# Fourier mixing followed by a leaky-ReLU layer: the head reordered, VectorE's order fixed, and the first d=128 row spread by TensorE

## The chip, the cores and the metric

The kernel runs on one core of one Trainium2 chip. A core has a matrix engine (TensorE, in the profile PE, with its weight loads as PEld), a vector engine (VectorE, DVE), an activation engine (ScalarE, ACT), GpSimd (POOL) and a queue engine (SyncE, SP) that here only issues DMAs. SBUF is the on-chip memory of 128 partitions; PSUM holds the sums that TensorE writes, and only VectorE and ScalarE empty it here. The engines run side by side, each in the order in which its instructions stand, and meet at semaphores. The metric is the device time of one execution in microseconds.

## What is computed

A batch of 8 sequences of 3008 rows and 256 features goes through a two-dimensional Fourier transform of which the real part is kept, and then through two matrices with a leaky ReLU between them:

```python
X = np.fft.fft(x, axis=1)          # along the 3008 rows of each of 8 sequences
X = np.fft.fft(X, axis=2)          # along the 256 features
x = X.real.reshape(24064, 256)
h = x @ w_in                       # 256 x 2048
g = np.maximum(0.01 * h, h)
out = g @ w_out                    # 2048 x 256
```

x is float32. The two weight matrices arrive as float64, which no engine here computes with: the kernel reads each number as two 32-bit words and puts a float32 together from them.

## The kernel before

The rows are transformed by matmuls with cosine and sine tables, after the symmetries of the transform have been used to shorten them: rows that mirror each other are added, columns d and 256-d are added (cosine part) and subtracted (sine part), and the two halves of the sequence are added for even frequencies and subtracted for odd ones. That is the fold of x. Column 128, which has no mirror, is kept apart for all 8 sequences as nyx and transformed once per parity; its row is then needed on all 128 partitions. The feature transform is not done at all on x: it is folded into w_in (up_ps = feature table times w_in), so that wf takes its place, and wn is the row of wf that belongs to column 128.

A unit is one sequence and one parity, odd first; a unit has three chunks of about 251 frequency pairs. F = 2048 hidden features are 16 blocks of 128. For each chunk and each pair of hidden blocks there is an up step (four matmuls, four VectorE operations, one leaky ReLU) and a down step. The first two chunks use plain down steps of eight matmuls with w_out alone; all later chunks use seven products with sums of w_out blocks (wt), made on GpSimd.

```python
B, S, D, F = 8, 3008, 256, 2048
P = 128
PARITIES = (1, 0)
UW = [753, 752]      # frequencies of a unit, by parity
CW = 251             # of a chunk
NF = F // P          # 16 hidden blocks
NH = NF // 2
WN = 512             # columns of one piece of w_in
WB = WN // D         # hidden blocks of one piece of w_out: 2
```

The fold of x:

```python
    def fold_rows(t, h):

        a, z = t[:, h, 0], t[:, h, 1]
        nc.vector.tensor_tensor(a, a, z, op=ALU.add)
        lo, hi = a[:, :, 1:P], a[:, :, P + 1 : D]
        nc.vector.tensor_tensor(z[:, :, P + 1 : D], lo, hi, op=ALU.subtract)
        nc.vector.tensor_tensor(z[:, :, 1:P], lo, hi, op=ALU.add)
        nc.scalar.copy(z[:, :, 0:1], a[:, :, 0:1])
        nc.gpsimd.memset(z[:, :, P : P + 1], 0.0)

    def fold_halves(b, t):

        a, z = t[:, :, 0], t[:, :, 1]
        nc.vector.tensor_tensor(a[:, 0], z[:, 0], z[:, 1], op=ALU.add)
        nc.vector.tensor_tensor(a[:, 1], z[:, 0], z[:, 1], op=ALU.subtract)
        zs[b] = t
```

The weights. raw is a buffer for the float64 words; begin takes mantissa and exponent apart, with ScalarE scaling the exponent, and end puts the float32 together (the constructor, which issues the load, and the branch for float32 weights are left out):

```python
    # ... class Weights
        def begin(self):
            hi = self.word(I32, 1)
            self.power = work.tile([P, WN], F32, tag="power", bufs=2, name="power")
            man, power = self.dst, self.power
            man_i, power_i = man.bitcast(I32), power.bitcast(I32)
            v = nc.vector
            v.tensor_scalar(man_i, in0=hi, scalar1=0xFFFFF, scalar2=0x100000, op0=ALU.bitwise_and, op1=ALU.bitwise_or)
            v.tensor_scalar(power_i, in0=hi, scalar1=20, scalar2=0x7FF, op0=ALU.logical_shift_right, op1=ALU.bitwise_and)
            nc.scalar.activation(power, power_i, ACT.Relu, scale=-1.0, bias=inf[:, 0:1])
            nc.scalar.activation(power_i, power, ACT.Relu, scale=-(2.0**23), bias=inf[:, 1:2])

        def end(self):
            hi, lo = self.word(I32, 1), self.word(U32, 0)
            man, power = self.dst, self.power
            man_i, power_i = man.bitcast(I32), power.bitcast(I32)
            v = nc.vector
            v.scalar_tensor_tensor(man, in0=lo, scalar=2.0**-32, in1=man_i, op0=ALU.mult, op1=ALU.add)
            v.scalar_tensor_tensor(power_i, in0=hi, scalar=-(2**31), in1=power_i, op0=ALU.bitwise_and, op1=ALU.bitwise_or)
            v.scalar_tensor_tensor(man, in0=man, scalar=2.0**-20, in1=power, op0=ALU.mult, op1=ALU.mult)

    def convert(made):
        for w in made:
            w.begin()
        for w in made:
            w.end()
```

The products of the feature table with w_in, the path of wn through DRAM, and the loads of w_out:

```python
    def load_w_in(f0):
        n, made = w_in.shape[1] // F, []
        for a in range(2):
            # ... src: 128 rows of w_in, columns f0 to f0 + WN
            made.append(Weights(src, w))
        return made

    def fold_w_in(f0, made):

        for w in range(2):
            pt = up_ps()
            for a in range(2):
                nc.tensor.matmul(pt, lhsT=feat_sb[:, a, w * P : (w + 1) * P], rhs=made[a].dst, start=(a == 0), stop=(a == 1))
            nc.scalar.copy(wf[:, w, f0 : f0 + WN], pt)

    def spread_wn(f0):

        row = wn_dram[:, f0 : f0 + WN]
        nc.scalar.dma_start(row.rearrange("(o h) n -> o h n", o=1), wf[0:1, 1].rearrange("o (h n) -> o h n", h=2)[:, :, f0 : f0 + WN])
        at = f0 // P

        def rest():
            for h in range(2):
                nc.scalar.dma_start(wn[:, h * NH + at : h * NH + at + WN // P], row[h].rearrange("(q p) -> p q", p=P))
        return rest

    def load_w_out(f):
        made = []
        for h in range(2):
            at = (h * NH + f) * P
            src = w_out[at : at + WB * P, :].rearrange("(c p) d -> p c d", p=P)
            made.append(Weights(src, wo[:, h, f : f + WB, :].rearrange("p c d -> p (c d)")))
        return made
```

Column 128: its transform is written to DRAM and read back as a row on all partitions.

```python
    def nyquist(c):
        # ... rows of column 128 by parity
        sums = sequence(rows, B, 0, c)

        def rest():
            t = work.tile([P, UW[0]], F32, tag="mix0", bufs=2, name="nyq")
            butterfly(t, sums, B, 0, c)
            nc.sync.dma_start(nyq_dram[:, c, 0 : UW[c]], t[0:B, 0 : UW[c]])
        return rest

    def spread(u):

        b, c = u
        t = work.tile([P, UW[0]], F32, tag="nb", bufs=2, name="nb")
        nc.sync.dma_start(t[:, 0 : UW[c]], nyq_dram[b, c, 0 : UW[c]].partition_broadcast(P))
        spreads[u] = t
```

The up step, and the order of steps. The down step of a step follows three steps later in the text of the program (lag = 3); a scheduler then orders each engine's instructions.

```python
    # ...
    plain = 2
    steps = [(j, f) for f in range(NH) for j in range(plain)]
    steps += [(j, f) for j in range(plain, len(blocks)) for f in range(NH)]

    def up(j, f):
        b, c, at, n, _ = blocks[j]
        pt = [up_ps("cos_ps"), up_ps("sin_ps")]
        for blk in range(2):
            for h in range(2):
                fs = slice((h * NH + f) * P, (h * NH + f + 1) * P)
                nc.tensor.matmul(pt[blk][:, h * n : (h + 1) * n], lhsT=wf[:, blk, fs],
                                 rhs=mixed[b, c][blk][:, at : at + n], start=True, stop=True)
        cos = work.tile([P, 2 * CW], F32, tag="cos", bufs=3, name="cos")
        for h in range(2):
            hs = slice(h * n, (h + 1) * n)
            nc.vector.scalar_tensor_tensor(cos[:, hs], in0=spreads[b, c][:, at : at + n],
                                           scalar=wn[:, h * NH + f : h * NH + f + 1],
                                           in1=pt[0][:, hs], op0=ALU.mult, op1=ALU.add)
        g = work.tile([P, 2 * WN], F32, tag="g", bufs=5, name="g")[:, 0 : 4 * n].rearrange("p (r k) -> p r k", r=2)
        nc.vector.tensor_tensor(g[:, 0], cos[:, 0 : 2 * n], pt[1][:, 0 : 2 * n], op=ALU.add)
        nc.vector.tensor_tensor(g[:, 1], cos[:, 0 : 2 * n], pt[1][:, 0 : 2 * n], op=ALU.subtract)
        nc.scalar.activation(g, g, ACT.Lrelu)
        a = [[g[:, r, h * n : (h + 1) * n] for h in range(2)] for r in range(2)]
        if j < plain:
            hidden[j, f] = a
            return
        # ... (sums on GpSimd for the later chunks)
```

The head, up to the point from which everything repeats:

```python
    # ...
    w0 = load_w_in(0)
    nc.sync.dma_start(feat_sb, feat_tab.rearrange("(a p) n -> p a n", p=P))
    w2 = load_w_in(2 * WN)
    nc.sync.dma_start(nyx, x_nyq)
    t0 = load_x(0)
    for n in range(4):
        load_tab(nc.sync, n, 1)
    convert(w0)
    fold_w_in(0, w0)
    convert(w2)
    fold_w_in(2 * WN, w2)
    spread_wn(0)()
    fold_nyquist()
    fold_rows(t0, 0)
    fold_rows(t0, 1)
    fold_halves(0, t0)
    nyquist(1)()
    dft(units[0], 0)()
    spread(units[0])
    dft(units[0], 1)()
    at = 0

    def some_steps(n):
        nonlocal at
        for _ in range(n):
            step(at)
            at += 1

    o = load_w_out(0)
    convert(o)
    some_steps(plain)
    w = load_w_in(WN)
    convert(w)
    fold_w_in(WN, w)
    some_steps(plain)
    w = load_w_in(3 * WN)
    convert(w)
    fold_w_in(3 * WN, w)
    spread_wn(WN)()
    some_steps(plain)
    o = load_w_out(WB)
    for n in range(4):
        load_tab(nc.sync, n, 0)
    convert(o)
    for blk in range(2):
        fold_x_quarters(0, blk)
    some_steps(plain)
    nyquist(0)()
    spread(units[1])
    for f in range(2 * WB, NH, WB):
        o = load_w_out(f)
        convert(o)
        some_steps(plain)
        dft(units[1], f // WB - 2)()
    for f in range(0, NH, WB):
        combine_w_out(f)
    some_steps(len(steps) + lag - at)
```

## Time and profile before

| what | value |
|---|---|
| time, median of 3 | 1936.75 us (1935.41 to 1936.89) |
| span of the profiled execution | 1935.4 us |
| TensorE busy | 1909.9 us, 99% |
| VectorE busy | 1149.3 us, 59% |
| GpSimd busy | 1055.4 us, 55% |
| ScalarE busy | 468.6 us, 24% |
| DMA moved | 73.68 MB, mean 38 GB/s |

A line of the profile names an engine, a line of the kernel (L491), the tile that is written and those that are read, and a shape: 128x251 is 128 partitions by 251 elements. A float32 matmul appears as two records, so a group of eight matmuls counts 16. The chain is the work that ended last, followed backwards: what each piece of it waited for. "issue" in it is time in which the profile shows nothing that the engine waited for. A matmul's end in the profile is a model; the distance from one start to the next is the surer measure.

### The profile page before, as it was taken

Reading aid. Unit: us, or ns where it says so; the run is one execution under the profiler, and the core shown is the slowest. Engines: PE = TensorE matmul, PEld = TensorE weight load, DVE = VectorE, ACT = ScalarE, POOL = GpSimd, SP = SyncE. Lnnn points to the kernel's source line nnn. Section 1 sums busy time; section 2 is a strip of 40 time slices with the busy share of each in tenths; the row PEclk is TensorE's granted clock in tenths of the full one; section 3 lists DMA queues with packets and bytes.
Section 4 is the critical chain, followed back from the end, with each engine's and each line's share of the span. In section 5 each row is a group of like instructions: output and inputs, shape, how many; then the busy total and the mean of one; then the engine's idle time right before and its main releaser. Section 6 shows DMA issues by size and latency. Waiting matters only on the chain.

```text
span 1935.4 us, 24654 instructions
## 1 busy us (share of the span) xinstructions
PE 1909.9 (99%) x8988; PEld 1687.9 (87%) x8988; DVE 1149.3 (59%) x2245; ACT 468.6 (24%) x560; POOL 1055.4 (55%) x1508
## 2 busy tenths in 40 slices
PE   5999999999999999999999999999999999999999
PEld 3888888888888888888888888888888888888888
DVE  7975555585455845567555775457645585545554
ACT  3522222222222222222222222222222222222221
POOL 0115555575555755557555665557655575555554
PEclk8999999999999999999999999999999999999999
DMA  7220000020001100020000200002000020000000
GB/s 276 63 87 30 11 20 11 22 95 11 19 22 68 39 12 30 12 88 19 22 19 11 95 20 14 19 11 96 22 11 19 11 106 11 18 13 22 11 11 22
DMA packets 25600, 73.68 MB, mean 38 GB/s; under 512 B 4596, under 2 KB 17524, under 8 KB 23432
## 3 DMA queue, kind: packets, MB, share of 16 engines
q1 hardware_dynamic: 23360, 72.09, 10.1%
q8 instruction: 72, 1.18, 0.2%
q14 instruction: 48, 0.39, 0.1%
q10 hardware_dynamic: 2120, 0.02, 0.1%
HBM read 47.38 MB, written 24.71 MB: 37 GB/s over the span
## 4 chain that ended last, share of the span: by engine, by line
PE 98%; DMA 1%; DVE 0%; issue 0%; ACT 0%; SPq 0%; ACTq 0%; DVEq 0%
PE sum_ps L554 56%; PE cos_ps L491 17%; PE sin_ps L491 17%; PE sum_ps L534 3%; PE dft_ps L412 3%; PE dft_ps L402 2%; PE up_ps L357 1%; DMA raw<-in_w_in_dram 0%; DMA wn_dram<-wf 0%; DVE power L333 0%; DVE e L565 0%; DVE cos L496 0%; ACT g L502 0%; ACTq L369 0%; SPq L305 0%
## 5 line engine op out<-in xcount | busy, mean ns | idle before, releaser
L496 DVE SCALAR_TENSOR_TENSOR cos<-nb,wn,cos_ps 128x251 f32<-128x251 f32 (+1 forms) x768 | 330.6, 472 | 682.6 <-PE cos_ps L491 682.3
L502 ACT ACTIVATE g<-g 128x1004 f32<-128x1004 f32 (+1 forms) x384 | 399.2, 1039 | 1154.4 <-DVE g L501 1102.6
L509 POOL TENSOR_TENSOR s<-g 128x251 f32<-128x251 f32 (+1 forms) x368 | 265.5, 721 | 727.1 <-ACT g L502 722.6
L554 PE MATMUL sum_ps<-s,wt 128*128 128x251 f32 (+1 forms) x2208 | 527.7, 374 | 0.0
L554 PEld LDWEIGHTS sum_ps<-s,wt 128*128 128x128 f32 x2208 | 416.3, 189 | 52.3
L491 PE MATMUL cos_ps<-mix,wf 128*128 128x251 f32 (+1 forms) x1536 | 388.1, 375 | 0.0
L491 PE MATMUL sin_ps<-mix,wf 128*128 128x251 f32 (+1 forms) x1536 | 387.7, 374 | 0.0
L554 PE MATMUL sum_ps<-g,wo 128*128 128x251 f32 (+1 forms) x1472 | 372.5, 375 | 0.0
L491 PEld LDWEIGHTS cos_ps<-mix,wf 128*128 128x128 f32 x1536 | 291.5, 190 | 36.0 <-issue 1.8
L491 PEld LDWEIGHTS sin_ps<-mix,wf 128*128 128x128 f32 x1536 | 290.6, 189 | 34.5 <-DVE mix L427 0.2
L554 PEld LDWEIGHTS sum_ps<-g,wo 128*128 128x128 f32 x1472 | 279.8, 190 | 38.4
L512 POOL TENSOR_TENSOR s<-g,s 128x251 f32<-128x251 f32 (+1 forms) x368 | 273.0, 742 | 28.9
L500 DVE TENSOR_TENSOR g<-cos,sin_ps 128x502 f32<-128x502 f32 (+1 forms) x384 | 259.5, 676 | 47.9 <-DVE cos L496 11.3
L510 POOL TENSOR_TENSOR s<-s,g 128x251 f32<-128x251 f32 (+1 forms) x368 | 271.4, 738 | 0.0
L511 POOL TENSOR_TENSOR s<-g 128x251 f32<-128x251 f32 (+1 forms) x368 | 263.6, 716 | 0.0
L501 DVE TENSOR_TENSOR g<-cos,sin_ps 128x502 f32<-128x502 f32 (+1 forms) x384 | 257.2, 670 | 0.0
L554 PE MATMUL sum_ps<-s,wo 128*128 128x251 f32 (+1 forms) x736 | 215.9, 375 | 0.0
L554 PE MATMUL sum_ps<-g,wt 128*128 128x251 f32 (+1 forms) x736 | 215.8, 375 | 0.0
L554 PEld LDWEIGHTS sum_ps<-s,wo 128*128 128x128 f32 x736 | 139.6, 190 | 16.2
L554 PEld LDWEIGHTS sum_ps<-g,wt 128*128 128x128 f32 x736 | 140.0, 190 | 15.7
L565 DVE TENSOR_TENSOR o<-e,sum_ps 128x251 f32<-128x251 f32 (+1 forms) x184 | 67.5, 408 | 8.7 <-ACT e L563 8.7
L534 PE MATMUL sum_ps<-g,wo 128*128 128x251 f32 x256 | 58.8, 383 | 2.9 <-ACT g L502 2.9
(65 smaller groups left out, 652.8 us busy)
## 6 DMA issues: line engine op xcount, KB each, us to landing
xt<-in_x_dram SPq DMA_DIRECT2D x16, 1792.0 KB, 6.8
out_dram<-o SPq DMA_DIRECT2D x80, 251.0 KB, 2.3
raw<-in_w_in_dram SPq DMA_DIRECT2D x8, 512.0 KB, 5.2
raw<-in_w_out_dram SPq DMA_DIRECT2D x8, 512.0 KB, 4.3
out_dram<-o SPq DMA_DIRECT2D x16, 250.0 KB, 2.3
nb<-nyq_dram SPq DMA_DIRECT2D x8, 376.5 KB, 3.3
nb<-nyq_dram SPq DMA_DIRECT2D x8, 376.0 KB, 4.4
tab<-in_seq_tab_dram SPq DMA_DIRECT2D x2, 564.0 KB, 13.9
```

The lines of the kernel that those rows point to most:

```text
L491: nc.tensor.matmul(pt[blk][:, h * n : (h + 1) * n], lhsT=wf[:, blk, fs], rhs=mixed[b, c][blk][:, at : at + n], start=True, stop=True)
L496: nc.vector.scalar_tensor_tensor(cos[:, hs], in0=spreads[b, c][:, at : at + n], scalar=wn[:, h * NH + f : h * NH + f + 1], in1=pt[0][:, hs ...
L500: nc.vector.tensor_tensor(g[:, 0], cos[:, 0 : 2 * n], pt[1][:, 0 : 2 * n], op=ALU.add)
L501: nc.vector.tensor_tensor(g[:, 1], cos[:, 0 : 2 * n], pt[1][:, 0 : 2 * n], op=ALU.subtract)
L502: nc.scalar.activation(g, g, ACT.Lrelu)
L509: nc.gpsimd.tensor_tensor(s1, a[1][0], a[1][1], op=ALU.add)
L510: nc.gpsimd.tensor_tensor(s2, s1, a[0][0], op=ALU.subtract)
L511: nc.gpsimd.tensor_tensor(s3, a[0][0], a[1][0], op=ALU.subtract)
L512: nc.gpsimd.tensor_tensor(s4, a[0][1], s2, op=ALU.subtract)
L534: nc.tensor.matmul(sums[j][d][:, r * n : (r + 1) * n], lhsT=wo[:, h, f, d * P : (d + 1) * P], rhs=a[r][h], start=(f == 0 and r == 0 and h ...
L554: nc.tensor.matmul(sums[j][p], lhsT=still[p], rhs=moving[p], start=(f == 0 and i % 2 == 0), stop=(f == NH - 1), skip_group_check=True)
L565: nc.vector.tensor_tensor(to, x, y, op=ALU.add)
```

## The change

The whole change lies in the head, apart from the way the fold of x is cut and the pairing of hidden blocks in the first two chunks. Its parts:

- The fold of x is cut into pieces by half (h), by part (0 cosine, 1 sine) and by parity (c), so that the first transform needs only the odd pieces.
- In the head, VectorE's instructions keep the order of the program's text (manual_schedule); the other engines are still ordered by the scheduler.
- The first two chunks pair neighbouring hidden blocks 2f and 2f+1 in place of f and 8+f. The first step then needs one piece of w_in and one of w_out, and w_out is loaded and converted in eighths, in order.
- The second piece of w_in is no longer loaded and converted ahead of x. The pieces of both matrices stand between pairs of steps.
- wn goes through DRAM in four parts on GpSimd's queue, in place of two on ScalarE's.
- The first row of column 128 is spread to all partitions by a matmul with a row of ones, in place of a trip through DRAM.
- A leaky ReLU of one column at the start makes ScalarE load its table there.

In the diff, a line of three dots stands where lines are cut: context, and removed lines that the kernel before shows above.

```diff
@@ -232,22 +232,37 @@
...
+    def add_mirrors(t, h):
 
         a, z = t[:, h, 0], t[:, h, 1]
         nc.vector.tensor_tensor(a, a, z, op=ALU.add)
+
+    def fold_columns(t, h, part):
+
+        a, z = t[:, h, 0], t[:, h, 1]
         lo, hi = a[:, :, 1:P], a[:, :, P + 1 : D]
...
+        if part == 0:
+            nc.vector.tensor_tensor(z[:, :, 1:P], lo, hi, op=ALU.add)
+            nc.scalar.copy(z[:, :, 0:1], a[:, :, 0:1])
+        else:
+            nc.vector.tensor_tensor(z[:, :, P + 1 : D], lo, hi, op=ALU.subtract)
+            nc.gpsimd.memset(z[:, :, P : P + 1], 0.0)
+
+    def fold_halves(t, part, c):
 
         a, z = t[:, :, 0], t[:, :, 1]
...
+        i, cols = (c + part) % 2, slice(part * P, (part + 1) * P)
+        nc.vector.tensor_tensor(a[:, i, :, cols], z[:, 0, :, cols], z[:, 1, :, cols], op=(ALU.add, ALU.subtract)[i])
+
+    def fold_x(b):
+        t = xs.pop(b)
+        for h in range(2):
+            add_mirrors(t, h)
+            for part in range(2):
+                fold_columns(t, h, part)
+        for part in range(2):
+            for c in PARITIES:
+                fold_halves(t, part, c)
...
@@ -279,7 +294,9 @@
...
-    wn_dram = dram.tile([2, F // 2], F32, name="wn_dram")
+    lrelu = const.tile([P, 1], F32, name="lrelu")
+    one = const.tile([1, P], F32, name="one")
+    wn_dram = dram.tile([F], F32, name="wn_dram")
...
@@ -321,15 +338,19 @@
...
+        def mantissa(self):
+            if self.f64:
+                man, lo = self.dst, self.word(U32, 0)
+                nc.vector.scalar_tensor_tensor(man, in0=lo, scalar=2.0**-32, in1=man.bitcast(I32), op0=ALU.mult, op1=ALU.add)
+
         def end(self):
...
+            hi = self.word(I32, 1)
             man, power = self.dst, self.power
...
+            power_i = power.bitcast(I32)
             v = nc.vector
...
@@ -338,6 +359,7 @@
     def convert(made):
         for w in made:
             w.begin()
+            w.mantissa()
         for w in made:
             w.end()
 
@@ -359,23 +381,15 @@
 
     def spread_wn(f0):
 
...
+        row = wn_dram[f0 : f0 + WN]
+        nc.gpsimd.dma_start(row.rearrange("(o n) -> o n", o=1), wf[0:1, 1, f0 : f0 + WN])
+        nc.gpsimd.dma_start(wn[:, f0 // P : (f0 + WN) // P], row.rearrange("(q p) -> p q", p=P))
+
+    def load_w_out(q):
+
+        src = w_out[q * WB * P : (q + 1) * WB * P, :].rearrange("(c p) d -> p c d", p=P)
+        h, f = divmod(q * WB, NH)
+        return [Weights(src, wo[:, h, f : f + WB, :].rearrange("p c d -> p (c d)"))]
...
@@ -464,6 +478,8 @@
         def rest():
             t = work.tile([P, UW[0]], F32, tag="mix0", bufs=2, name="nyq")
             butterfly(t, sums, B, 0, c)
+            if c == PARITIES[0]:
+                spread_first(t)
...
@@ -473,6 +489,17 @@
...
+
+    def spread_first(rows):
+
+        c = PARITIES[0]
+        t = work.tile([P, UW[0]], F32, tag="nb", bufs=2, name="nb")
+        for i in range(2):
+            half = slice(i * UW[c] // 2, (i + 1) * UW[c] // 2)
+            pt = dft_ps()[:, 0 : UW[c] // 2]
+            nc.tensor.matmul(pt, lhsT=one, rhs=rows[0:1, half], start=True, stop=True)
+            nc.scalar.copy(t[:, half], pt)
+        spreads[0, c] = t
 
 
...
@@ -482,19 +509,23 @@
     steps = [(j, f) for f in range(NH) for j in range(plain)]
...
+    def hidden_blocks(j, f):
+
+        return (2 * f, 2 * f + 1) if j < plain else (f, NH + f)
+
     def up(j, f):
         b, c, at, n, _ = blocks[j]
+        fs = hidden_blocks(j, f)
         pt = [up_ps("cos_ps"), up_ps("sin_ps")]
         for blk in range(2):
             for h in range(2):
...
-                nc.tensor.matmul(pt[blk][:, h * n : (h + 1) * n], lhsT=wf[:, blk, fs],
+                nc.tensor.matmul(pt[blk][:, h * n : (h + 1) * n], lhsT=wf[:, blk, fs[h] * P : (fs[h] + 1) * P],
                                  rhs=mixed[b, c][blk][:, at : at + n], start=True, stop=True)
...
             nc.vector.scalar_tensor_tensor(cos[:, hs], in0=spreads[b, c][:, at : at + n],
-                                           scalar=wn[:, h * NH + f : h * NH + f + 1],
+                                           scalar=wn[:, fs[h] : fs[h] + 1],
                                            in1=pt[0][:, hs], op0=ALU.mult, op1=ALU.add)
...
@@ -527,11 +558,11 @@
...
-        a = hidden.pop((j, f))
+        a, fs = hidden.pop((j, f)), hidden_blocks(j, f)
         for d in range(2):
             for r in range(2):
                 for h in range(2):
-                    nc.tensor.matmul(sums[j][d][:, r * n : (r + 1) * n], lhsT=wo[:, h, f, d * P : (d + 1) * P], rhs=a[r][h],
+                    nc.tensor.matmul(sums[j][d][:, r * n : (r + 1) * n], lhsT=wo[:, fs[h] // NH, fs[h] % NH, d * P : (d + 1) * P], rhs=a[r][h],
                                      start=(f == 0 and r == 0 and h == 0), stop=(f == NH - 1 and h == 1), skip_group_check=True)
...
@@ -580,10 +611,7 @@
...
+                        fold_x(b + 1)
...
@@ -593,28 +621,6 @@
...
@@ -623,32 +629,70 @@
...
+    with tc.manual_schedule(engines={mybir.EngineType.DVE}):
+        nc.vector.memset(inf[:, 0:1], 1151.0)
+        nc.vector.memset(inf[:, 1:2], 255.0 * 2.0**23)
+        nc.gpsimd.memset(one, 1.0)
+
+        nc.scalar.activation(lrelu, inf[:, 0:1], ACT.Lrelu)
+        w = load_w_in(0)
+        nc.sync.dma_start(nyx, x_nyq)
+        nc.sync.dma_start(feat_sb, feat_tab.rearrange("(a p) n -> p a n", p=P))
+        t = load_x(0)
+        for n in range(4):
+            load_tab(nc.sync, n, 1)
+        o = load_w_out(0)
+        convert(w)
+        fold_w_in(0, w)
+        spread_wn(0)
+        fold_nyquist()
+        for h in range(2):
+            add_mirrors(t, h)
+            fold_columns(t, h, 0)
+        zs[0] = t
+        fold_columns(t, 1, 1)
+        fold_halves(t, 0, 1)
+        rest = nyquist(1)
+        fold_columns(t, 0, 1)
+        rest()
+        fold_halves(t, 1, 1)
+        rest = dft(units[0], 0)
+        w = load_w_in(WN)
+        for part in o:
+            part.begin()
+            part.mantissa()
+        rest()
+        dft(units[0], 1)()
+        some_steps(1)
+        for part in o:
+            part.end()
+        some_steps(1)
+        convert(w)
+        fold_w_in(WN, w)
+        spread_wn(WN)
+        o = load_w_out(1)
         convert(o)
         some_steps(plain)
...
+        for n in range(4):
+            load_tab(nc.sync, n, 0)
+        for q in range(2, NF // WB):
+            o = load_w_out(q)
+            convert(o)
+            if q % 2 == 0:
+                w = load_w_in(q // 2 * WN + WN) if q // 2 * WN + WN < F else []
+                convert(w)
+                if w:
+                    fold_w_in(q // 2 * WN + WN, w)
+                    spread_wn(q // 2 * WN + WN)
+            if q in (2, 3):
+                fold_halves(t, q - 2, 0)
+            if q in (4, 5):
+                fold_x_quarters(0, q - 4)
+            rest = {5: lambda: nyquist(0), 6: lambda: dft(units[1], 0), 7: lambda: dft(units[1], 1)}.get(q, lambda: lambda: None)()
+            some_steps(plain)
+            rest()
+            if q == 5:
+                spread(units[1])
     for f in range(0, NH, WB):
         combine_w_out(f)
     some_steps(len(steps) + lag - at)
```

## The prediction

> **What bounds the kernel now.** I first read busy times and the chain that ended last on the profile's page.
>
> ```profile
> PE 1909.9 (99%) x8988; PEld 1687.9 (87%) x8988; DVE 1149.3 (59%) x2245; ACT 468.6 (24%) x560; POOL 1055.4 (55%) x1508
> PE 98%; DMA 1%; DVE 0%; issue 0%; ACT 0%; SPq 0%; ACTq 0%; DVEq 0%
> ```
>
> TensorE (PE) is the bound, and 25.5 us of the span (1935.4 - 1909.9) is all it sits still. The second view, busy time by stretch, says where. After span and PE, its columns are PE loads, VectorE (DVE), ScalarE, GpSimd, granted PE clock, DMA share and GB/s.
>
> ```profile
> 0.00:20.00 20.00, 9.05 (x15) 3.97 (x16) 14.14 (x30) 8.93 (x15) 0.32 (x5) 1.00 0.90 354
> 20.00:40.00 20.00, 12.67 (x43) 7.81 (x42) 15.46 (x27) 6.36 (x14) 0.11 (x1) 0.74 0.63 211
> 40.00:60.00 20.00, 17.14 (x63) 12.79 (x62) 18.05 (x38) 8.76 (x13) 2.82 (x4) 0.91 0.44 154
> 60.00:80.00 20.00, 20.00 (x88) 16.28 (x87) 19.88 (x45) 9.29 (x13) 3.01 (x4) 1.00 0.29 80
> ```
>
> From 60 us on PE is never idle, so only the first 60 us can give anything. VectorE is full at 60 to 80 us: it converts the float64 weights while it feeds the first chunks. The third view, the chain in order of time (start, length, what), shows the head:
>
> ```profile
> 2.11 6.53 DMA raw<-in_w_in_dram
> ...
> 10.95 9.95 PE up_ps L357 x16
> 20.90 0.02 issue
> 20.92 0.59 ACT wf L358
> 21.51 0.02 issue
> 21.54 4.27 DMA wn_dram<-wf
> ...
> 27.14 4.33 issue
> 31.48 2.85 PE dft_ps L402 x8
> ...
> 47.15 8.33 PE sum_ps L534 x30
> ```
>
> The 4.33 us called issue is VectorE: it folds both halves of x, even and odd frequencies, 27.44 to 31.4. ScalarE waits 4.27 us for its own small DMA before it copies the nyquist sums. Dense work begins at 47.15. The last view is the timeline, for durations:
>
> ```profile
> 16.58 2.02 DVE L239 TENSOR_TENSOR xt<-xt 128x1792 f32<-128x1792 f32 x1
> 18.68 1.07 DVE L241 TENSOR_TENSOR xt<-xt 128x889 f32<-128x889 f32 x1
> 46.05 1.04 ACT L502 ACTIVATE g<-g 128x1004 f32<-128x1004 f32 x1 [5.46 <-DVE g L501]
> 69.38 3.56 PE L534 MATMUL sum_ps<-g,wo 128*128 128x251 f32 x16
> DMA to landing us min/median/max: 11.0/12.6/14.3
> ```
>
> The last line is of the two halves of x, issued at about 3.6 and 4.7: they land at 14.6 and 18.9.
>
> **What the Trainium skill says.** "TensorE: Matmul & The Clock Gate", What's actually happening: the array runs at half clock until it has been busy for a window of about 3.4 us, and falls back after an idle one. The trace agrees: 512-column passes start 0.85 us apart until 16.86 us, then 0.43; after idling from 24.15 to 31.48 the 188-column passes take 0.36 again, later 0.16. "VectorE: DVE Perf Modes", The perf-mode tier table: a float32 tensor_tensor runs at one element per cycle, so pieces cost about what the whole did: 1792 elements take 2.02 us, 889 take 1.07. "ScalarE: Activation LUTs", What ACT_TABLE_LOAD costs: about 1283 ns; the trace has two of 1.28 us. The change moves the second, at 39.31 us, to the start; ScalarE had no leaky ReLU before 46.05, so it brings nothing. "DMA: Bandwidth & Descriptors", Issuing engines are not separate DMA queues: all issuers share 16 engines. So moving the w_n trip to GpSimd frees ScalarE's queue but does not speed the trip.
>
> **The change, part by part.** Starts of one after another on VectorE, from the timeline: bit operations of a conversion 0.34, its other three 0.60; 0.13 more where the next needs the last at once; fold of 1792 elements 1.93, of 889 or 896 0.99; one chunk step (two scalings, add, subtract) 2.14. ScalarE: each exponent step 0.75, leaky ReLU 1.04. PE: 128x251 matmul 0.425 (16 passes in 3.40), up step 1.70, plain down step 3.40, projection of one w_in piece 3.42, odd transform of a block 3.13, even 1.89.
>
> 1. The second w_in piece (two loads, 1.0 MB) leaves the front. At about 0.4 MB/us x lands 2.6 us earlier: 12.0 and 16.3. Its two conversions, about 5 us of VectorE ahead of x, go too.
>
> 2. Fold: x half 0 at 12.05 to 15.0, then x half 1 from 16.4: add 1.93, columns 0.99 and 0.99, odd cosine fold 0.99, other columns 0.99, nyquist butterfly about 1.6, giving 23.9; odd sine fold to 24.9. Before, both halves for both parities and ScalarE's wait took until 31.4.
>
> 3. First d=128 spread: two one-row matmuls of 376 columns, 1.25 us of PE that did not exist, on the way at about 23.4. In place of a DRAM trip that landed at 39, four microseconds ahead of its first use at 43.0: no gain of its own here, but needed once everything is earlier.
>
> 4. Two odd transforms, 6.27 us: 24.5 to 30.9. Butterfly to 31.8; two chunk steps interleaved with the end of w_out's first eighth. Neighbouring blocks make that one eighth (and one w_in piece) enough for the first down product; before, two eighths and two pieces were. First down product at 35.5 instead of 47.15: 11.6 us earlier.
>
> 5. The work put off comes back. Full-speed matmul work done at the start of dense work: before 6.84 + 9.4 + 3.4 = 19.65 of 47.15 us, 27.5 lost; after 3.42 + 9.4 + 1.25 + 3.4 = 17.5 of 35.5, 18.0 lost. Now three pieces of w_in (5.25 us of VectorE each) and seven eighths of w_out (3.65 each, of which 1 us waits on ScalarE's exponents) stand in a fixed order between pairs of chunk steps. Followed down the order of both engines, PE runs dry here: 0.85 us before the second pair's down products; 2.55 before the third piece's projection (PE done at 56.35, VectorE's piece at 58.9); 2.2 before the fourth (82.7 against 84.9); 0.9 at the fifth pair; 0.65 at the even nyquist transform; about 1 at the sixth pair, where that transform still holds two of the four PSUM buffers. Together some 7.5 us by 120 us. Before, counted the same way at 109.94 us: 13.7 + 15.1 + 20.4 + 30.6 = 79.8 of work, 30.1 lost, so only 2.6 after dense start.
>
> Sum: 30.1 - (18.0 + 7.5) - 1.25 = 3.3 us gained. From 120 us on nothing is saved: the fold of later batches in ten pieces is as long as in eight (11.8 against 11.7 us) and PE never waits there. x of the second batch is read about 9 us later (its predecessor is released at 118.5 instead of 110) but its first fold has moved with it.
>
> The clock: PE idles from about 20.6 to 23.4 before the spread, 2.8 us, just under the window. Before, a stretch of 7.3 us cost it. If it falls to half, the 7.5 us that follow cost 1.7 to 3 us more; at even chances about 1.1. That leaves 2.2, or 1934.5. My hand table gives every wait its full length and trusts no overlap, so I put the time slightly lower: **1933.5 us**.
>
> **Rivals.** (a) The head gain survives: PE does not run dry because VectorE's order, chosen by hand, fits better than my table. For: VectorE was 99% full at 60 to 80 before, yet PE lost nothing there. Against: before, conversions stood between chunk steps one operation at a time, and here they stand in blocks of 5 to 9 us, more than two chunk steps' 10.2 us of PE allow once a projection is due. It would make 1926 to 1928. (b) The fixed order costs more than the head brings. For: VectorE is serial from 32 to 107 us, so each extra microsecond there is PE's; operations on two SBUF tensors stretch where GpSimd works (0.93 instead of 0.41 for a 256-element one at 139.03), and GpSimd's 32 weight combinations of 0.73 fall in the same stretch. Against: they did so before as well. It would make 1937 to 1940. (c) The w_n trip on GpSimd becomes the wait: issued about 16.5 behind the first projection, two trips of 4.3 and 4.8 us (ScalarE's figures) end near 27, first use 31.9; GpSimd's in-order queue also holds a memset of x behind it that VectorE wants at 23.8. Slack 5 and 1.5 us. If GpSimd issues slowly, 1936.
>
> **Range and chances.** Removing every microsecond of idle time in the head would give 25 us, 1.3%, so over 2% faster is out of reach; 2% slower would need 39 us of new stalls in work that touches only the first 120 us. 1927 to 1939 covers (a) almost whole and most of (b). Chances: faster 0.01, same 0.98, slower 0.01.
>
> **What would show it.** Right: in the chain in time order, first down products near 35 us; VectorE's first fold near 12; stretches between 55 and 95 us in which PE is less than full, ended by VectorE's converted w_in; from 120 on PE full. Step 5 is wrong if PE is full from 36 us (then a gain near 10); step 1 if the fold starts where it did; step 4 if dense work starts after 40; the clock guess by the granted clock at 23 to 31 us. The prediction is wrong if PE shows any idle time beyond 120 us, which I have given none.

## The result, and the profile after

The changed kernel takes **1945.22 us** (median of four runs, 1943.81 to 1946.40) against 1936.75 before (four runs, 1935.41 to 1936.89): a ratio of 1.0045, 95% interval 1.0028 to 1.0062. It is slower by 0.45%, 8.5 us. The prediction was 1933.5 us with a range of 1927 to 1939; the result lies 6 us outside it.

The page of the changed kernel, busy times and the chain that ended last:

```profile
PE 1914.9 (99%) x8992; PEld 1686.5 (87%) x8992; DVE 1160.1 (60%) x2261; ACT 470.9 (24%) x562; POOL 1066.9 (55%) x1517
PE 95%; DVE 3%; DMA 1%; ACT 1%; issue 0%; SPq 0%; DVEq 0%
```

PE is busy 5 us longer than before and 29.2 us of the span (1944.1 - 1914.9) it sits still, 3.7 us more than before. So there are two losses of about equal size: more waiting, and work that takes PE longer (1.25 us of it is the new spread, the rest is slower work). The chain now holds 3% of VectorE where it held none. Busy time by stretch (columns as in the prediction's view) tells where:

```profile
20.00:40.00 20.00, 16.37 (x49) 11.10 (x48) 11.81 (x25) 3.48 (x7) 0.91 (x2) 0.74 0.51 184
40.00:60.00 20.00, 18.78 (x79) 14.94 (x80) 17.38 (x34) 10.04 (x14) 2.80 (x4) 1.00 0.39 106
60.00:80.00 20.00, 17.69 (x76) 13.90 (x75) 16.07 (x29) 8.57 (x14) 3.65 (x4) 1.00 0.35 106
80.00:100.00 20.00, 16.62 (x57) 11.37 (x56) 14.03 (x28) 7.49 (x10) 3.31 (x4) 0.83 0.08 26
100.00:120.00 20.00, 17.44 (x89) 13.67 (x88) 15.12 (x35) 5.99 (x8) 3.41 (x4) 1.00 0.02 1
120.00:140.00 20.00, 20.00 (x99) 17.58 (x99) 16.66 (x32) 6.56 (x10) 4.25 (x7) 1.00 0.47 177
```

Before, PE was full from 60 us on; now it runs dry until 120 us, and VectorE, which before was 99% busy at 60 to 80, is at 80% there and at 70% from 80 to 100. The engine that was to be the limit of this stretch stands idle in it. The clock is 0.74 at 20 to 40 us, and 0.83 at 80 to 100.

The chain in order of time (start, length, what) shows both losses in single lines:

```profile
23.52 2.84 PE dft_ps L500 x4
26.36 2.81 PE dft_ps L416 x8
29.16 3.76 PE dft_ps L426 x6
32.92 1.31 PE dft_ps L416 x8
34.23 1.91 PE dft_ps L426 x6
...
64.46 3.70 PE up_ps L379 x8
...
92.04 6.51 PE up_ps L379 x8
```

L416 and L426 occur twice, for the first and the second block of the odd transform, with the same shapes: 2.81 and 3.76 us in the first, 1.31 and 1.91 in the second. With the spread (2.84 against the 1.25 it costs at full clock) the half clock took 1.59 + 1.50 + 1.85 = 4.9 us. The fourth piece's projection took 6.51 us where the third's took 3.70: 2.8 us more. What stood ahead of the slow ones is in the timeline of PE and, the longest of its kind, a wait of PE between 36 and 125 us:

```profile
18.25 2.06 PE L426 MATMUL dft_ps<-tab,nyx 128*8 128x376 f32 x6
23.52 2.84 PE L500 MATMUL dft_ps<-nyq,one 1*128 1x376 f32 x4 [3.21 <-DVE nyq L441]
...
40.79 1.51 PE L565 MATMUL sum_ps<-g,wo 128*128 128x251 f32 x6 [1.21 <-DVE wo L355]
```

```profile
PE up_ps L379 <- DVE win L355: 5.7, 2, 3.4
```

PE waits 3.21 us for the nyquist butterfly before the spread, and up to 3.4 us for a converted piece of w_in (L355 ends a conversion) before a projection (L379). After each of these two longest waits the clock is at half. VectorE's idle time in this part is mostly the other side of the same thing: between 60 and 100 us it waits 6.9 us for up products (L522), which stand behind the late projections in PE's queue, and 2.4 us for ScalarE's exponents.

To compare kernels I sum what PE loses: for each matmul the time to the start of the next, less what its columns take at full rate (0.212 us for 251). On this count the old kernel had lost 27.4 us by 45 us and 30.2 by 125; the changed one 23.3 by 45 and 37.3 by 125. So the head did gain 4.1 us, though 4.9 us of half clock are in it, and the stage after it lost 14.0 us where the old kernel lost 2.8. The spread adds 1.25 us of work. 37.3 + 1.25 - 30.2 = 8.35 of the 8.7 us by which the two profiled spans differ: nothing is left for what comes after 125 us.

### The profile page after: what moved, and what is told of

It reads as the page before. It is cut to its first block, busy times and chain, and to the rows that moved or that the text cites. A ratio compares the mean times of both kernels' runs of the same rounds, so it can differ in the third digit from the quotient of the medians.

```text
span 1944.1 us, 24669 instructions
## 1 busy us (share of the span) xinstructions
PE 1914.9 (99%) x8992; PEld 1686.5 (87%) x8992; DVE 1160.1 (60%) x2261; ACT 470.9 (24%) x562; POOL 1066.9 (55%) x1517
## 4 chain that ended last, share of the span: by engine, by line
PE 95%; DVE 3%; DMA 1%; ACT 1%; issue 0%; SPq 0%; DVEq 0%
PE sum_ps L585 56%; PE cos_ps L522 16%; PE sin_ps L522 16%; PE dft_ps L426 3%; PE dft_ps L416 2%; PE sum_ps L565 1%; DMA xt<-in_x_dram 1%; PE up_ps L379 1%; DVE cos L527 0%; DVE g L531 0%; DVE power L354 0%; DVE g L532 0%; ACT g L533 0%; DVE wo L355 0%; DVE win L344 0%; ACT power L339 0%
## 5 line engine op out<-in xcount | busy, mean ns | idle before, releaser
L527 DVE SCALAR_TENSOR_TENSOR cos<-nb,wn,cos_ps 128x251 f32<-128x251 f32 (+1 forms) x768 | 330.6, 472 | 674.3 <-PE cos_ps L522 674.2
L522 PE MATMUL sin_ps<-mix,wf 128*128 128x251 f32 (+1 forms) x1536 | 387.8, 374 | 0.3 <-DVE g L532 0.3
L522 PE MATMUL cos_ps<-mix,wf 128*128 128x251 f32 (+1 forms) x1536 | 388.0, 375 | 0.1
L522 PEld LDWEIGHTS cos_ps<-mix,wf 128*128 128x128 f32 x1536 | 291.2, 190 | 36.8 <-issue 2.1
L522 PEld LDWEIGHTS sin_ps<-mix,wf 128*128 128x128 f32 x1536 | 290.2, 189 | 35.7 <-PE cos_ps L522 0.7
L541 POOL TENSOR_TENSOR s<-s,g 128x251 f32<-128x251 f32 (+1 forms) x368 | 277.5, 754 | 0.0
```

The source lines that it names most:

```text
L541: nc.gpsimd.tensor_tensor(s2, s1, a[0][0], op=ALU.subtract)
```

## Theories and experiments

Two things are to be explained: the waits from 45 to 120 us with the idle VectorE, and the two falls of the clock. My theory: (1) VectorE's fixed order, in which conversions stand in blocks between the chunk steps, and not the amount of work put off, makes PE run dry; (2) the clock falls because of the gaps ahead of it, of which the first comes from the place of the spread matmuls in PE's queue. The rivals: the work put off is too much for VectorE by 110 us whoever orders it; the one-row matmuls or something else than the gap bring the clock down.

Times are medians; each ratio is to runs of the kernel before on the same chip (1936.3, 1936.3 and 1937.1 us in the three groups of runs).

### VectorE's order left to the scheduler

```diff
-    with tc.manual_schedule(engines={mybir.EngineType.DVE}):
+    if True:
```

> The changed kernel with one part undone: VectorE's order is again the scheduler's, not that of the text. Theory (the fixed order, with conversions in blocks, makes TensorE run dry in the plain stage): of the 9.8 us that PE loses to waits between 52 and 117 us some 5 to 8 come back, and the second fall of the clock (2.9 us at 92 us) is gone: 1936 to 1939 us. Rival (the work put off is simply too much for VectorE before 110 us, whoever orders it): 1944 to 1947 us, the losses at other places.

**1931.16 us**, ratio 0.9974 (0.9964 to 0.9984): 14 us faster than the changed kernel, 5 us faster than the old one. By stretch:

```profile
60.00:80.00 20.00, 19.70 (x86) 15.92 (x85) 19.91 (x43) 10.35 (x15) 5.64 (x7) 1.00 0.20 55
80.00:100.00 20.00, 20.00 (x101) 16.70 (x100) 18.41 (x36) 8.21 (x12) 8.34 (x11) 1.00 0.09 22
```

The same work, and PE is full; VectorE is 98% busy and more from 40 to 80 us (19.62 us of the stretch from 40 to 60) and has time to spare after 100. Between 45 and 125 us PE loses 1.6 us instead of 14.0. I had expected 5 to 8 us from the waits plus 2.9 from the clock, 1936 to 1939 us; it came out faster than that, because nearly all of these losses went and the head, where VectorE's order is another one too, lost some 2 us less. The rival falls: the work fits. The clock still falls in the head, after a gap of 4.0 us ahead of the spread.

### PE kept busy before the spread

```diff
         rest = nyquist(1)
+        warm = ps.tile([P, 512], F32, tag="sum", bufs=4, name="warm")
+        for i in range(5):
+            nc.tensor.matmul(warm[:, 0:376], lhsT=feat_sb[:, 0, 0:P], rhs=tabs[1, 1][:, 0:376], start=True, stop=True)
         fold_columns(t, 0, 1)
```

> The changed kernel with five more matmuls of 128x376, whose sums nobody reads, put between the odd nyquist transform and the two one-row spread matmuls, where PE otherwise sits still from 20.2 to 23.5 us. They take about 3.1 us of PE in that gap. Theory (a gap of 3.4 us halves the clock from 24 to 32 us and costs 4.9 us): granted clock 1.0 in that stretch, L500 at 1.25 us instead of 2.84, first block's transform 3.1 instead of 6.5, first down product near 36 us, 1940 to 1941 us. Rival (the clock falls for another cause, such as the one-row matmuls, or VectorE is the wait there anyway): clock still about 0.5, 1944 to 1946 us.

**1944.71 us** (1941.87 to 1945.0), ratio 1.0037 (1.0024 to 1.005). PE's timeline:

```profile
22.00 3.43 PE L658 MATMUL warm<-tab,feat_sb 128*128 128x376 f32 x10
25.35 1.53 PE L500 MATMUL dft_ps<-nyq,one 1*128 1x376 f32 x4
26.81 1.54 PE L416 MATMUL dft_ps<-tab,xt 95*128 95x188 f32 x8
```

The same one-row matmuls and the same transform run at full rate when no gap stands ahead of them, so the fall needs the gap, and the one-row matmuls do not bring it alone (what part they have in it is in the last section). But the time hardly moved. The filler ran late (the nyquist transform was itself at half clock here), so the first down product came at 38.07, 2.7 us earlier and not 4.9. And the lead shrank behind it: the gap before the third piece's projection was as long as in the changed kernel (2.5 us), this time the clock fell after it, and by the fourth projection 1.1 us of the lead were left. Part (2) holds as to the gap; the sum I expected did not, because a fixed order behind the head decides what a lead is worth.

### The spread through DRAM again

```diff
-            if c == PARITIES[0]:
-                spread_first(t)
...
+        spread(units[0])
         rest = dft(units[0], 0)
```

> The changed kernel with one part undone: the first d=128 spread goes through DRAM again instead of through two one-row matmuls on TensorE. Theory (the spread matmuls stand in PE's queue ahead of the first block's transform and make the gap that halves the clock): the first transform follows the nyquist one after about 1 us, the clock stays at 1.0, L500's work is gone, 1937 to 1941 us, unless the spread lands after about 30 us and VectorE waits for it. Rival (the spread on TensorE is what lets the first chunks start; without it they wait for the DRAM trip of some 8 us): first down product as late as 40 us or later, 1944 to 1948 us.

**1938.53 us** (20 runs, 1936.25 to 1943.13), ratio 1.0016 (1.0009 to 1.0023). Now the first transform follows the nyquist one, and the up steps are done 7 us earlier. PE's timeline:

```profile
22.19 1.54 PE L416 MATMUL dft_ps<-tab,xt 95*128 95x188 f32 x8
...
28.64 1.01 PE L520 MATMUL cos_ps<-mix,wf 128*128 128x251 f32 x4
...
35.23 9.60 PE L563 MATMUL sum_ps<-g,wo 128*128 128x251 f32 x30 [2.98 <-DVE wo L355]
```

The rival falls: first down products come 5.6 us earlier than in the changed kernel, not later. But VectorE does wait for the DRAM trip, though its timeline names another cause:

```profile
31.53 0.86 DVE L525 SCALAR_TENSOR_TENSOR cos<-nb,wn,cos_ps 128x251 f32<-128x251 f32 x2 [1.69 <-PE cos_ps L520]
```

The up products named (28.64) were done at 29.7 us; the spread was issued at 25.8 and landed 5.6 us later, at 31.4, just ahead of this first use. So some 1.6 us of VectorE's standing still are the trip's. What the first down products wait for is the end of w_out's first eighth, which the fixed order puts behind that chunk step; this gap brings the clock down again (30 records take 9.60 us; at full rate 30 take 6.6). So only 3.9 us of this execution's span are gained; the median of all runs is 6.7 us below the changed kernel.

### Conversions split by halves, close to their use

```diff
-        convert(w)
-        fold_w_in(WN, w)
-        spread_wn(WN)
...
-                convert(w)
-                if w:
-                    fold_w_in(q // 2 * WN + WN, w)
-                    spread_wn(q // 2 * WN + WN)
...
-            some_steps(plain)
+            some_steps(1)
...
+                convert(halves[0:1])
+            some_steps(1)
...
+                convert(halves[1:2])
+                fold_w_in((q + 1) // 2 * WN, halves)
+                spread_wn((q + 1) // 2 * WN)
```

(The second, third and fourth piece are so treated, in the second, fourth and sixth pair of steps.)

> The changed kernel with the conversions of the second to fourth w_in piece placed differently in VectorE's fixed order: half a piece between two chunk steps, one pair of steps earlier than their first use rather than two or more, and one eighth of w_out ahead of each pair. Theory (blocks of 5 to 9 us of conversion make PE wait for a projection that nothing needs yet): the waits at 61.8 and 88.3 us (2.5 and 3.5 us) and the second fall of the clock (2.9 us) vanish, 1936 to 1938 us. Rival (VectorE's total work sets it, so the wait moves to another place): 1943 to 1946 us, PE losses between 50 and 120 us still near 13 us in sum.

**1954.01 us**, ratio 1.0090 (1.0075 to 1.0106): worse by 9 us than the changed kernel. VectorE's waits between 36 and 118 us:

```profile
DVE power L354 <- ACT power L339: 11.0, 9, 1.6
DVE cos L527 <- DMA wn<-wn_dram: 7.2, 2, 5.1
```

I had overlooked two things. A piece is usable only after its w_n has made two DMA trips, and I left no time for them: 5.1 us of waiting in one place. And there is a wait I had not counted as one: ScalarE's two exponent steps in each conversion.

### The projection alone moved

```diff
                 convert(w)
-                if w:
-                    fold_w_in(q // 2 * WN + WN, w)
-                    spread_wn(q // 2 * WN + WN)
...
             some_steps(plain)
+            if q % 2 == 0 and w:
+                fold_w_in(q // 2 * WN + WN, w)
+                spread_wn(q // 2 * WN + WN)
```

VectorE's instructions stand in the same order as in the changed kernel.

> The changed kernel with VectorE's order untouched and only TensorE's moved: the projections of the third and fourth w_in piece (and their w_n trips) stand behind the chunk steps of the pair instead of ahead of them. Theory A (PE loses time because its in-order queue holds a projection that nothing needs yet, with chunk steps ready behind it): the waits at 61.8 and 88.3 us and the second fall of the clock go, 1936 to 1938 us. Theory B (while VectorE converts for 5 to 9 us without a chunk step, the down products have no input either): the wait only moves from L379 to L565, sums of PE loss 60 to 100 us still 6 us or more, 1941 to 1945 us.

**1939.55 us**, ratio 1.0022 (1.0015 to 1.0029), but scattered from 1937.3 to 1946.7 over 19 runs. Of PE's waits from 15 to 130 us the longest is:

```profile
PE up_ps L379 <- DVE cos L527: 4.9, 2, 2.7
```

This is neither theory as I wrote it. Time fell by 5.7 us as A wants, but the waits are still there, 2.9 and 2.4 us of loss instead of 2.5 and 3.5: now the projection waits until VectorE's chunk step (L527) has freed its PSUM buffer, and that chunk step stands behind the same block of conversions. So B is right about the mechanism: the block starves PE whatever stands in its queue. What improved the profiled execution is for the most part the clock: neither gap brought it down, and in the head, where nothing was changed, it was at half for 3.4 us in place of 10.2. That is luck and not the edit; the scatter of 9 us between executions says how much is left to chance here.

### Halves again, with a pair's time to spare

```diff
-                convert(w)
-                if w:
-                    fold_w_in(q // 2 * WN + WN, w)
-                    spread_wn(q // 2 * WN + WN)
...
-            some_steps(plain)
+            some_steps(1)
+            for a in w[0:1] if q % 2 == 0 else []:
+                convert([a])
+            some_steps(1)
+            if q % 2 == 0 and w:
+                convert(w[1:2])
+                fold_w_in(q // 2 * WN + WN, w)
+                spread_wn(q // 2 * WN + WN)
```

> The changed kernel with the third and fourth w_in piece converted by halves between the two chunk steps of a pair, and projected at the end of that pair, which leaves one whole pair (about 10 us) for the projection and the two w_n trips before the first use; the earlier splitting left none, and VectorE then waited 5 us for w_n. Theory B (long blocks of conversion starve PE, whatever stands in its queue): PE loss between 55 and 100 us falls from 9 to about 3 us, 1937 to 1939 us. Theory A (the projection's place is all): the same as with the projection moved alone, within 1.5 us. If even this stays at 1943 or more, a fixed order of this kind does not fit VectorE's work at all.

**1945.04 us**, ratio 1.0045 (1.0030 to 1.0060): no gain at all. The waits for w_n are gone, the blocks are shorter, and yet VectorE stands still as long as in the changed kernel (16.4 us of waits against 16.8), only for another cause. Its waits between 36 and 118 us for the exponents, and for up products in the changed kernel, where these are the longest; first the changed kernel, then this one, then the scheduler's order:

```profile
DVE cos L527 <- PE cos_ps L522: 9.6, 3, 4.5
DVE power L354 <- ACT power L339: 5.8, 5, 1.2
```

```profile
DVE power L354 <- ACT power L339: 11.5, 9, 2.1
```

```profile
DVE power L354 <- ACT power L339: 0.4, 1, 0.4
```

A conversion sends its exponent to ScalarE and cannot end before it is back. Two conversions in one block hide each other's trip; a single one in a fixed order stands still for it, as this timeline shows:

```profile
89.12 0.68 DVE L344 SCALAR_TENSOR_TENSOR win<-raw,win 128x512 f32<-128x512 uint32 x1
91.01 0.69 DVE L354 SCALAR_TENSOR_TENSOR power<-raw,power 128x512 int32<-128x512 int32 x1 [1.20 <-ACT power L339]
```

By splitting I had made the blocks shorter and the trips more exposed. That gave a sharper theory, C: what the fixed order loses is VectorE's own idle time beside ScalarE's exponent steps, and a fixed order that puts a chunk step into each trip would be as good as the scheduler's.

### A chunk step inside each exponent trip

```diff
-            o = load_w_out(q)
-            convert(o)
...
+            start(o + w[0:1])       # bit operations and mantissa
...
-            some_steps(plain)
+            some_steps(1)
+            finish(o + w[0:1])      # the two operations that need the exponent
+            start(w[1:2])
+            some_steps(1)
+            finish(w[1:2])
+            if w:
+                fold_w_in(q // 2 * WN + WN, w)
+                spread_wn(q // 2 * WN + WN)
```

> The changed kernel, VectorE's order still fixed, but no conversion stands whole between chunk steps any more: the bit operations and mantissa of one or two weights stand ahead of a chunk step, their two last operations behind it, so that ScalarE's exponent steps run beside the chunk step; projections stand at the end of the pair. Theory C (besides the projection's place, what a fixed order loses is VectorE standing still for ScalarE's exponents: 5.8 us of waits in the changed kernel, 8.1 with the projections late, 11.5 with halves split, 0.4 in the scheduler's order): these waits fall below 2 us, PE loss between 50 and 120 us to about 4 us, 1934 to 1937 us. Rival (ScalarE's exponents are not what counts): 1939 us or more, as with the projections late alone.

**1932.52 us** (1930.17 to 1934.81), ratio 0.9977 (0.9967 to 0.9987). The waits for exponents are gone: VectorE has a single kind left between 36 and 118 us,

```profile
DVE cos L536 <- PE cos_ps L531: 6.4, 3, 2.7
```

that is, it now waits for PE rather than PE for it, and by stretch:

```profile
60.00:80.00 20.00, 19.90 (x86) 15.55 (x85) 19.55 (x38) 10.74 (x16) 3.15 (x4) 1.00 0.33 106
```

PE loses 3.3 us between 45 and 125 us where the changed kernel lost 14.0. It was better than I expected. That the order is fixed is thus not what costs, but what the order leaves uncovered. That the exponent trips are the uncovered part, theory C, fits but is not isolated: this edit also shortens the blocks and moves the projections, and VectorE's waits for up products fell too, from 9.6 to 6.4 us. Late projections alone kept both of PE's waits, and shorter blocks with late projections but without covered trips brought nothing; no run has covered trips alone.

### The first transform ahead of the spread

The spread stays on TensorE; only the first block's transform is put before it:

```diff
         rest = nyquist(1)
+        first = dft(units[0], 0)
         fold_columns(t, 0, 1)
         rest()
         fold_halves(t, 1, 1)
-        rest = dft(units[0], 0)
+        rest = first
```

With the covered fixed order just shown:

> The same fixed order as the one before, with the first block's odd transform ahead of the spread matmuls as well. Theory (two independent losses, the clock in the head and the fixed order after it, each with its own cure): 3 to 5 us below the one before, 1929 to 1933 us, close to the scheduler's order with the same head (1927). Rival (an earlier head is eaten by the fixed order, as with the filler matmuls): within 1.5 us of the one before.

**1928.84 us** (1928.69 to 1929.06), ratio 0.9958 (0.9943 to 0.9973), 3.7 us below the one before it. With the scheduler's order:

> The changed kernel with VectorE's order the scheduler's, and the first block's odd transform put ahead of the two spread matmuls in TensorE's queue; the spread stays on TensorE. Theory (the gap of 3.4 to 4 us ahead of the spread is what halves the clock, and the transform fills it): clock 1.0 from 20 to 32 us, first down product about 4 us earlier than with the scheduler's order alone, 1926 to 1928 us. Rival (VectorE's folds, not PE, end the head): 1930 to 1932 us, and PE is idle elsewhere before 36 us instead.

**1926.99 us** (1926.84 to 1927.14), ratio 0.9952 (0.9937 to 0.9967): 18 us below the changed kernel and 9.3 below the old one, the lowest median of all. PE's timeline:

```profile
22.28 1.51 PE L416 MATMUL dft_ps<-tab,xt 95*128 95x188 f32 x8 [0.18 <-issue]
23.62 2.06 PE L426 MATMUL dft_ps<-tab,xt 128*128 128x376 f32 x6
25.61 1.53 PE L500 MATMUL dft_ps<-nyq,one 1*128 1x376 f32 x4
...
35.13 3.03 PE L565 MATMUL sum_ps<-g,wo 128*128 128x251 f32 x13 [1.00 <-ACT g L533]
```

The transform fills the gap, the spread follows at full rate without a wait, and the first down product comes at 35.13 us. Once VectorE's order starves PE no more, the head's cure gives about the same in either order, 4.2 us in the scheduler's and 3.7 in the covered one. Ahead of the blocks of conversions, the filler's gain in the head was eaten.

### The parts of the head under the scheduler's order

The spread through DRAM and VectorE's order left to the scheduler, the two diffs above together:

> The changed kernel with two parts undone: VectorE's order is the scheduler's, and the first d=128 spread goes through DRAM. Theory (the spread matmuls cost their own 1.25 us and, by the gap ahead of them, some 3.3 us of half clock): clock 1.0 from 20 to 32 us, 1926 to 1928 us. Rival (the spread's landing near 32 us becomes the wait, as 3.1 us of it was under the fixed order): 1929 to 1932 us, with a gap before the first down product.

**1927.69 us**, ratio 0.9955 (0.9941 to 0.9970). The time is as expected, the clock is not: 0.83 at 20 to 40 us. A gap of only 2.0 us after the nyquist transform was followed by half clock until 26.5 us. Some 2 us of the first down product's wait are for its ReLU, not for the DRAM trip, which lands at 30.5 us, 1.5 us ahead of its first use (under the fixed order some 1.6 us of waiting were the trip's, not the 3.1 that I wrote above). The result lies 0.7 us above the version with the transform first, and the two intervals overlap: that a spread by TensorE is worth anything over the trip through DRAM is not shown.

The filler matmuls and VectorE's order left to the scheduler:

> The changed kernel with VectorE's order the scheduler's and with the five filler matmuls of 128x376, whose sums nobody reads, ahead of the spread matmuls. Measures the clock's share alone where nothing behind it eats the gain: the scheduler's order without filler lost 3.3 us by half clock at 25 to 32 us. Theory: 1927 to 1929 us. If VectorE ends the head rather than PE: 1930 to 1932 us.

**1929.57 us** (1928.77 to 1931.26), ratio 0.9963 (0.9950 to 0.9976). In the profiled execution, the fastest of five, the clock is 1.00 throughout 20 to 40 us and VectorE is busy for all of that stretch, so VectorE ends the head here; the filler gives 1.6 us, not 3.3.

The best version with x folded whole, as in the old kernel:

```diff
-        for h in range(2):
-            add_mirrors(t, h)
-            fold_columns(t, h, 0)
-        zs[0] = t
...
+        xs[0] = t
+        fold_x(0)
         rest = nyquist(1)
         first = dft(units[0], 0)
-        fold_columns(t, 0, 1)
         rest()
-        fold_halves(t, 1, 1)
...
-            if q in (2, 3):
-                fold_halves(t, q - 2, 0)
```

> The best version so far (scheduler's order on VectorE, first block's transform ahead of the spread, 1927.0 us) with one part of the change undone: x of the first batch is folded whole again, even frequencies too, before the nyquist butterfly. Two extra fold operations (2 us of VectorE) come ahead of the first chunk. Theory (the pieces only move 2 us of VectorE work out of the head): 1928 to 1929.5 us. Rival (the early x and the fewer weights at the front bring it all, the pieces nothing): 1926.5 to 1927.5 us.

**1929.10 us**, ratio 0.9958 (0.9944 to 0.9972): with the pieces it was 2.1 us less. Not all of it need be the two fold operations: here too a gap of 2.0 us ahead of the transform was followed by half clock, until 26 us.

## Why the prediction was wrong

**Steps 1 and 2 held.** x half 0 is folded from 11.44 us (predicted 12.05), half 1 from 15.89 (16.4); the spread starts at 23.52 (23.4).

**Step 3 was wrong in its second half.** The spread costs what I said at full clock. But "needed once everything is earlier" did not come true as meant: with the DRAM trip, VectorE waits some 1.6 us for it in the fixed order and not at all in the scheduler's, and in both the kernel is faster than with the spread where I had it. Where it stood in PE's queue it did harm, because it made the transform behind it wait for the nyquist butterfly, though that transform's input was ready (L255 ends at about 21.2 us). I worked out that the transform would start at 24.5 without asking why it should stand behind the spread.

**Step 4 was late almost by its clock alone.** First down product at 40.79 instead of 35.5: 4.9 us of half clock. Without these, lost PE time at the end of the head is 23.3 - 4.9 = 18.4 us; predicted 18.0.

**The clock guess is the term that failed.** I had put the first gap at 2.8 us "just under the window" and taken even chances of 1.7 to 3 us, 1.1 us in the sum. It lost 4.9 us there and 2.8 a second time, which I had not considered although my own table had waits of 2.55 and 2.2 us: 7.7 us in all, 6.6 us more than in the sum. The gap itself was 3.4 us, as the nyquist transform had ended earlier than I reckoned. But "just under the window" was the wrong test in any case: the traces have falls after gaps of 2 us, because what goes with a fall is how little PE works within a fixed stretch of 3.41 us (last section).

**Step 5 was close in its table and wrong in its cause.** Waits of 0.85, 2.55, 2.2, 0.9, 0.65 and about 1 us were predicted; I put them at 7.5 us together, but they add up to 8.15. Measured: 0.6, 2.5, 3.5, 1.0, 1.4 and 0.8, together 9.8. Ahead of the 3.5, VectorE operations took about twice as long where GpSimd summed weights (last section). So rival (b), "the fixed order costs more than the head brings", was the right one, and I had weighed it lower. But the heading of the step, "the work put off comes back", is refuted: with the same work put off and the scheduler's order, 1.6 us are lost between 45 and 125 us. I had counted "1 us waits on ScalarE's exponents" into the cost of each eighth of w_out as if it were work of VectorE; it was idle time that another order fills.

**The sum.** Predicted 1934.5 by hand. 6.6 us more for the clock, 2.3 for the waits (0.65 of it my slip in adding them up), 0.4 in the head, and some 1.4 us of losses too small to have been in the table make 10.7: 1945.2, the measured time. The last 1.0 us of the miss I added myself, when I put the time below my sum because it "trusts no overlap". In this fixed order there was little overlap to trust.

**Rival (a)**, the head's gain surviving at 1926 to 1928 us, is what the change gives when both losses are cured: 1927.0. **Rival (c)** fell in the changed kernel (VectorE does not wait for w_n), but appeared when one experiment left the trip no time: 5.1 us. Beyond 125 us PE is full, as predicted.

## What to carry to other kernels

When the order of an engine is fixed by hand, look at that engine's own idle time first: here VectorE went from 99% to 80% busy in the stretch that it was meant to carry. It waited for ScalarE's exponents, and still longer for PE, which had itself waited for VectorE's block of conversions. Put other work into each trip from VectorE to ScalarE and back, keep the blocks short, or leave the order to the scheduler and set only what it gets wrong. In front of a matmul engine, look for the instruction that waits while one behind it is ready: one transform moved ahead of two small matmuls was worth 4 us. And a predicted gap of 2 us or more on PE carries a clock risk of several us, wherever it stands (21 of 25 such gaps here were followed by half clock). Where a trace names the cause of a wait, look whether that cause was not long done: the DRAM trip stood behind the name of a matmul.

## What the hardware showed

**The clock goes by fixed stretches of time, not by the length of a gap.** "TensorE: Matmul & The Clock Gate", What's actually happening, calls the window of about 3.4 us free-running, and so the switching variable from run to run; its table in Why this matters for your kernels advises against idle gaps above some 3 us. The traces bear out the first: in the clock record of each of the 14 traces, every stretch of full or half clock up to the kernel's end lasts a whole multiple of 3.413 us, and the boundaries lie elsewhere in each execution. They show the second to be too generous. From 19 us on, PE has 25 gaps of 2.0 us or more in these traces; 21 were followed by half clock, those of 2.4, 2.5, 2.9 and 3.5 us were not. What decides is how a gap lies between the boundaries. Here are such stretches whole, PE's busy time behind the span, the clock third from the right; the first is of the changed kernel, the next three of the DRAM spread:

```profile
19.22:22.63 3.41, 1.09 (x4) 0.16 (x2) 3.30 (x5) 0.00 (x0) 0.91 (x2) 1.00 1.04 416
```

```profile
58.37:61.78 3.41, 1.20 (x6) 0.74 (x4) 3.38 (x8) 2.78 (x4) 0.00 (x0) 1.00 0.28 107
85.68:89.09 3.41, 2.01 (x10) 1.46 (x8) 3.41 (x6) 1.44 (x2) 2.77 (x3) 1.00 0.00 0
89.09:92.50 3.41, 1.44 (x4) 0.73 (x5) 3.34 (x6) 1.44 (x2) 0.00 (x0) 1.00 0.22 71
```

After the first, with 1.09 us of work, the clock fell at 22.63 us, before the spread had begun. In the DRAM spread the gap of 2.5 us lies within one stretch, which leaves 1.20 us of work, and the clock fell; the gap of 3.5 us is cut in two by a boundary, which leaves 2.01 and 1.44, and it did not. The covered fixed order has a fall after a gap of 1.0 us only:

```profile
23.46:26.87 3.41, 2.69 (x11) 1.58 (x11) 3.03 (x6) 1.27 (x3) 0.00 (x0) 1.00 0.24 55
26.87:30.29 3.42, 3.42 (x9) 2.24 (x9) 0.85 (x3) 1.33 (x3) 0.00 (x0) 0.50 1.02 329
```

PE was busy for 2.69 us of the first, but 1.4 us of this was the one-row spread. If each matmul's time counts by the share of the 128 rows that it uses, this stretch has 31% and not 79%. On this count, in the first 160 us of all 14 traces, the 28 full-clock stretches before a fall have 43% at most and the 513 that no fall followed 42% at least (by plain busy time, 79% and 42%); full clock came back only after a stretch of 83% or more. So a stretch need not be idle for the clock to fall after it, and the one-row matmuls hardly count as work: in the changed kernel the stretch from 22.63 to 26.05 us, with nothing but the spread in it, counts 1%, and half clock lasted until 32.87. This rule is read from the traces of this kernel, with modelled ends of matmuls; no run was made to test it.

The times of one kernel scatter accordingly: by 6.9 us with the DRAM spread and by 9.4 with late projections, but by 0.3 and 0.4 in the two versions with the first transform ahead of the spread. The mean clock granted to each execution is on record, and goes with its time. With the DRAM spread, six executions at 1.000 took 1936.25 to 1936.99 us, eight at 0.996 and 0.997 took 1941.18 to 1943.13; with late projections, eight at 0.998 took 1937.30 to 1939.02, six at 0.994 and 0.995 took 1943.14 to 1946.74.

**VectorE stretches beside GpSimd, not only where it reads two tensors.** In the changed kernel, VectorE's timeline and GpSimd's in the same microseconds:

```profile
86.42 0.42 DVE L336 TENSOR_SCALAR win<-raw 128x512 int32<-128x512 int32 x1
86.76 0.95 DVE L337 TENSOR_SCALAR power<-raw 128x512 int32<-128x512 int32 x1
87.63 1.22 DVE L344 SCALAR_TENSOR_TENSOR win<-raw,win 128x512 f32<-128x512 uint32 x1
```

```profile
86.65 0.78 POOL L399 TENSOR_TENSOR wt<-wo,wt 128x256 f32<-128x256 f32 x1 [7.74 <-DVE wo L355]
```

The bit operation of one tensor and constants takes 0.95 us instead of 0.42, the mantissa with two tensors 1.22 instead of 0.69: half a microsecond more each. "SBUF — State Buffer", SBUF: two separate sides, says that the two engines share one pair of ports, held for a whole instruction, and that a VectorE operation takes it with two inputs from SBUF or in a faster mode of two ports. That agrees: undisturbed, the bit operation on 512 elements starts 0.34 us before the next one, the two-tensor operation of the same size 0.60. The prediction had named only the two-tensor kind. Three such operations, 1.6 us in excess, lie ahead of the fourth projection, whose wait was 1.3 us longer than predicted. That the one makes the other was not tried.
